# First parameters and last reads on two DMA queues, last rows in four groups, row tables of the last stage on GpSimd

## The chip, the cores and the metric

The kernel runs on one core of a Trainium2 chip. The metric is the time of one execution on the device, in microseconds, and its median over the runs. A core has five engines that work side by side: TensorE (PE; its weight loads are PEld), VectorE (DVE), ScalarE (ACT), GpSimd (POOL) and SyncE (SP). SP issues transfers, ACT can issue them too; sixteen DMA engines carry them out.

## The reference, cut to what matters

```python
def reference(A_u, ..., gate_w):                 # x = A_u: [1, 2048, 640], bf16
    x = A_u
    g = sigmoid((x * gate_w).sum(-1, keepdims=True))
    a = A_ref(x, ...)                            # long convolution, below
    b = (gelu(x @ w_gate) * (x @ w_up)) @ w_down # w_gate, w_up: [640, 1728]
    return g * a + (1 - g) * b

def A_ref(u, A_re, A_im, B_re, B_im, C_re, C_im, log_dt, Dskip):   # [640, 128] each
    dt = exp(log_dt)[:, None]
    logdA, dB = dt * (A_re + 1j * A_im), dt * (B_re + 1j * B_im)
    P = exp(logdA[:, :, None] * arange(2048)[None, None, :])
    K = einsum("dn,dnl,dn->dl", C_re + 1j * C_im, P, dB).real      # one filter per channel
    y = irfft(rfft(u, 4096) * rfft(K, 4096))[:2048]                # along the sequence
    return y + u * Dskip
```

## The kernel before, in words

The kernel does four things at once on five engines, and a written list sets the order.

**The filter.** `A_log_dt` and six parameter tables (`AreT`, `AimT`, `CreT`, `BreT`, `CimT`, `BimT`, 160 KB each) are loaded; ACT makes `dtT` = exp(`ldtT`) (L494), DVE makes `aT` (L495), `aN` (L737) and `bK` (L497). From these ACT makes exponentials (`exps1`, L647; `exps2`, L675) and sines (L633) of phases that DVE computes (`phases`, L624, L626, L628); DVE multiplies them into two grids (L661 to L662, L679, L685), and PE contracts the grids into the filter (`contract`, L711). This is done for each half of the 640 channels (`kgen(0)`, `kgen(1)`), and the result goes to the DRAM tile `dS`.

**The transforms.** The convolution is a Fourier transform in two stages of matrix products. The tables of sines and cosines, `WA`, `TB` and, for the last stage, `WAT`, are made by ACT from integer phases. The phases need per-partition numbers (row numbers with their bits in another order), which DVE computes from the partition number in single-column instructions: `fields` (L367, used by all), `rows` (L387, for `WA`) and `last_rows` (L400, for `WAT`). `WAT` itself comes from an iota on POOL (L949), a DVE instruction (L950) and ACT (L952). The first stage of the input is L776 (16 blocks `un`, results to the DRAM tile `dU`), that of the filter L840 (its rows gathered from `dS` by L804 and L812, results to `dKA`). The second stage is `stageB` (L867), in eight pieces `c` of four columns. `product` (L888) multiplies the two spectra, and `inverse` (L899) transforms each piece back and writes it to the DRAM tile `dY` (L907). `dY` has three parts: `dY[0]` (64 rows) holds the pieces 0 to 3, `dY[1]` (32 rows) 4 and 5, `dY[2]` (32 rows) 6 and 7.

**The last stage** is `finish` (L910). Eight tiles `g` of four columns are read back from `dY` (L913), each in three transfers, since the partitions of a tile come from three parts of `dY`: every second partition from part 0 (320 KB), every fourth from 1 and 2 (160 KB each). Per tile there are two output blocks `ph`. For each, PE does eight products (L922) and DVE computes `z = ps * g + z` (L927). Each tile is then written out in two transfers (L931).

**The feed-forward part.** `gate` (L544 on PE, gelu on ACT L548), `up` (L564 on PE, product on DVE L568) and the down projection `downs` (L592, 28 products for one of sixteen blocks, evicted with the scale 1 - g by L261 or L265), in two groups of 1024 rows. The weights come in blocks of 160 KB through three buffers each (L465), the input `xT` in four loads of 640 KB (L468). Each PSUM result has a pair of banks of its own, of which there are four.

**What sets the order.** Every step is added to a plan (`add`, L98) with its engine, what it reads and writes, and a cost and a rank, which are notes for a planner and aren't used in the kernel. `emit` (L130) goes through the list `ORDER` (L27). One number holds the step, its engine and its pair of PSUM banks:

```python
            s = self.steps[v // 20]
            s["eng"] = ("PE", "DVE", "ACT", "POOL", "SP")[v % 20 // 4]
            s["k"] = 2 * (v % 4)
```

So `ORDER` fixes the order on each engine, and whether an eviction runs on ACT (L259, L261) or DVE (L263, L265). All transfers are issued by SP (`dma`, L242), each engine and SP in the order of the list: an issue that waits holds up all that stand behind it on that queue.

At the end of the list SP issues the writes of pieces 0 to 4, the eight reads of part 0, the writes of the pieces 7, 5 and 6, then the sixteen reads of parts 1 and 2, mixed, and sixteen output writes. PE's last down projections stand between the last inverses; two stand behind the last of them, ahead of L922.

Of the kernel before, what the change touches and what calls it, by code (L numbers as in the profile page):

```python
# [8 lines left out]
ALU = mybir.AluOpType  # L9
# [18 lines left out]
    12 336 6316 316 536 436 516 396 1432 24 376 692 676 988 416 496 476 456 356 616 1004 576 636 1564 556 44 1628  # L28
    656 736 936 596 1064 816 756 2740 1608 64 956 776 716 836 876 1104 1588 796 916 1044 976 2861 1024 896 2836 84
    856 1648 1664 2982 2956 2768 1084 4383 1724 3076 3008 104 2780 2888 1164 1688 4404 1124 1442 1501 2856 2903 1144  # L30
    2804 1748 1784 2976 3020 2924 128 3096 1208 1464 6323 9384 6362 1496 1524 6436 1704 3341 1556 4428 1188 1228
    6388 6348 3436 3222 3044 3368 6416 1764 3103 3316 3248 1808 3380 3196 4444 1844 6441 3456 3262 6468 3404 1868
    1824 6481 3336 3700 6556 6508 3128 6536 1244 3461 3796 3284 3728 144 3143 3556 3488 1884 1268 6562 3216 6600
    3581 6676 6588 6628 1284 168 6656 1304 3822 3676 1324 1344 3608 3500 3916 3848 6721 3576 6748 6682 6796 1364
    6708 4181 3524 6776 1388 3164 3942 4276 4208 1404 2124 6840 4036 6803 3968 3861 6916 6868 2184 6828 2008 3622
    6896 3936 1904 3740 3696 2088 2024 3884 1928 6963 3816 3764 6921 6988 7036 2104 2048 3980 3644 6948 2064 1968
    4063 7016 1944 4056 4004 2148 4222 1984 4156 184 7081 264 4296 7040 2208 7156 2244 7108 7068 4301 2224 288 7136
    208 4088 224 4376 4244 7200 4328 7163 7224 4102 7276 7188 4344 248 7256 2164 4176 4124 2268 7280 2304 7323 4501
    7396 7348 7308 2284 7376 2328 2364 4702 4528 9484 2388 7443 7400 2344 4661 7516 7428 7468 2404 9508 7496 9544
    4728 2420 4688 9604 7523 2444 7562 7548 2461 7636 7588 7616 2503 2484 7640 2524 7682 7668 2541 7756 7708 4580  # L40
    2564 9408 7736 7803 9468 4604 7762 4461 7876 7784 7824 9524 9448 7856 2580 2622 9788 4743 4484 2644 9428 9804
    2604 9828 2716 7881 4764 7922 2676 4620 7996 7904 7948 2736 2696 9844 9908 7976 9748 9924 8556 4543 4644 9868
    8436 8376 9764 8236 8456 9568 9884 8576 8516 8536 8416 8256 8041 4564 8476 8002 4900 8496 8024 8116 8068 8316
    9664 9628 8296 8096 5023 8396 4996 8336 9584 8276 4928 8356 4782 5116 5048 9644 8121 4876 4808 8160 5063 8148
    8188 9688 9944 8216 5382 5136 5141 5476 5084 9968 9704 8620 5236 8583 8608 8648 4823 10064 5408 8676 4940 4896
    5168 4844 10004 8682 5016 8721 8708 5423 8748 8776 4964 10028 5182 5496 5444 9984 5261 5256 5204 10088 8820
    10124 5356 8783 5742 8808 8848 5503 5288 10184 5836 8876 5620 5768 5596 9724 11236 5528 11016 10044 8921 5648
    5716 5302 8948 10104 10148 8883 5324 5376 5540 8904 8976 5781 5564 5616 10208 10164 11322 11283 5856 11020 11348
    11304 11048 8982 5804 9023 9008 5660 9048 10224 9076 11142 11456 10241 5684 11168 5736 11243 11362 10264 10360
    11268 11388 9083 10384 9121 9108 11582 9144 11460 11608 11103 11484 11061 9176 11128 11542 11676 11564 11500  # L50
    11088 10323 12116 11524 9182 10344 9221 9208 10280 9248 9276 11682 11803 10304 11656 11721 11708 11416 11748
    11216 12242 11824 11196 12200 12268 12121 11636 12224 9283 11436 12148 9322 11896 9304 9348 10400 10441 10424
    9376 12163 11762 10468 12184 6080 11788 10536 10496 11856 10516 11876 5861 6108 12316 12296 10556 5983 5956 5888
    12616 12756 6122 6008 6076 11900 11941 6144 11983 11928 11968 12020 12004 5902 12476 12048 12336 13176 13216
    13256 13236 6161 5924 13336 13436 13196 13376 5976 12663 12620 6188 6242 12684 13296 13516 12644 13416 13356
    12724 13276 12343 13496 12481 6268 12704 12520 12096 13316 12364 12508 13396 13456 6284 12548 12383 6201 13476
    12408 12896 12584 13036 12076 12424 13620 12444 13522 13648 13563 13544 13588 12800 12828 12564 13723 13616
    13662 13748 6224 12760 14556 13688 12943 12964 12788 13081 13716 13042 13108 13064 12900 13763 14336 12928 13821
    13124 13862 13788 6020 12984 13888 13816 13144 13848 13004 13916 13963 10892 14642 6044 13921 13988 13948 14683
    14664 14560 14708 14601 14016 14584 14916 14462 14628 14343 14776 14484 14368 14020 14061 14048 10904 14123  # L60
    14382 14148 14084 14160 14188 14263 14404 14116 14221 14288 15180 14216 14244 14962 14756 15208 15263 14736
    14984 14921 15288 14316 15500 14944 14422 15528 10643 14444 10928 12844 14536 14516 12864 10952 15004 14781
    14820 10668 15024 10842 15376 15056 14848 10964 15696 14808 16016 10988 14884 14864 15823 10864 15420 15381
    15848 16656 15404 15102 15448 15063 16336 15124 15088 15581 15700 15608 15464 15743 10562 16976 15728 15164
    15768 15144 15804 15784 15484 15221 10588 15860 15244 15303 15888 15622 15324 16021 15648 15540 16044 15568
    16063 15356 16342 17296 16088 16364 15940 15676 15901 15968 16383 16104 10682 15928 16404 15996 16444 16424
    16124 16140 10704 16221 16168 16183 16244 16262 16208 17340 16284 17368 17021 16463 17048 16484 16500 16316
    16542 16528 16581 16564 16663 16608 16700 16684 16862 16728 16636 16781 16884 17303 16808 10720 17324 17384
    17676 17756 16764 17736 17404 17696 17656 16744 17716 17422 10748 17616 17541 17444 17503 17636 17568 16900
    17524 17182 16928 17461 17204 17103 17488 16820 17124 16982 16848 17596 10601 17004 16956 17084 17064 17143  # L70
    10624 17220 17168 10762 17244 17276 17796 17916 10801 10784 17856 17876 17776 17936 17996 17976 17956 18016
    18056 10824 17836 18083 18076 18120 18104 17816 18036 18144 18202 17896 18241 18563 18224 18196 18600 18176
    18264 18482 18504 18441 18316 18296 18464 18682 18624 18961 18556 18536 18584 18920 18944 18363 18676 18656
    18704 18720 18744 18802 18824 18320 18796 18776 18984 18842 18864 19036 19016 18384 18916 18896 18344 18416
    18436
# [81 lines left out]
def kernel(  # L157
# [72 lines left out]
    def mm(n):  # L230
        return n / 2.28 + 4
# [10 lines left out]
    def dma(kb, fn, r=(), w=(), rank=5.0, run=1280, **k):  # L242
        return add({"SP": 450}, lambda s: fn(), r, w, rank=rank, lat=1900, x=max(100, kb * (3.7 if run < 1000 else 3.3 if run < 2500 else 2.9)), **k)
# [94 lines left out]
    dY = [dp.tile([n, 32, D], BF16, name=f"dY{q}") for q, n in enumerate((64, 32, 32))]  # L338
# [24 lines left out]
    pool(2800, iotas, w=["iot", "ones", "ci"])  # L363

    FIELDS = ((0, 1), (1, 15), (5, 1), (1, 31), (1, 1), (2, 31), (0, 127), (2, 1), (3, 15), (1, 63), (4, 7), (3, 1))

    def fields():  # L367
# [5 lines left out]
        v.tensor_copy(out=ff[:, 0:12], in_=fi[:, 0:12])  # L373
# [7 lines left out]
    B0, B1, B2, B3, P1, P2, P3, P4 = [ff[:, c:c + 1] for c in (0, 4, 7, 11, 9, 5, 8, 10)]  # L381

    def select(v, out, cond, a, b):
        v.tensor_scalar(out=sc8[:, 15:16], in0=a, scalar1=b, scalar2=None, op0=ALU.subtract)
        v.tensor_scalar(out=out, in0=sc8[:, 15:16], scalar1=cond, scalar2=b, op0=ALU.mult, op1=ALU.add)
# [14 lines left out]
    def last_rows():  # L400
        v = nc.vector
        v.tensor_scalar(out=sc8[:, 8:9], in0=B1, scalar1=8.0, scalar2=P4, op0=ALU.mult, op1=ALU.add)
        v.tensor_scalar(out=sc8[:, 8:9], in0=sc8[:, 8:9], scalar1=16.0, scalar2=None, op0=ALU.add)
        select(v, sc8[:, 6:7], B0, sc8[:, 8:9], P3)
        select(v, sc8[:, 9:10], B0, B3, B2)
        select(v, sc8[:, 10:11], B0, B2, B1)
        v.tensor_scalar(out=sc8[:, 9:10], in0=sc8[:, 9:10], scalar1=1024.0, scalar2=8.0, op0=ALU.mult, op1=ALU.add)
        v.tensor_scalar(out=sc8[:, 6:7], in0=sc8[:, 6:7], scalar1=32.0, scalar2=sc8[:, 9:10], op0=ALU.mult, op1=ALU.add)
        v.tensor_scalar(out=sc8[:, 3:4], in0=sc8[:, 10:11], scalar1=-16384.0, scalar2=16384.0, op0=ALU.mult, op1=ALU.add)
# [631 lines left out]
```

## Time and profile before

| What | Value |
|---|---|
| runs, us | 313.37, 312.61, 317.1, 313.4, 313.98, 311.93 |
| their median | 313.38 us |
| profiled execution | 311.22 us, span 309.4 us |
| busy, share of the span | PE 84%, DVE 80%, ACT 72%, POOL 2% |
| granted clock of TensorE, mean | 0.95 |
| DMA | 60.62 MB in 45859 packets, mean 196 GB/s, 61.1% of 16 engines' span, all on one queue |
| loads of ACT's function tables | 26, of 1283 ns each |
| first matmul | 10.34 us |
| last write of `dY`: issued, landed | 280.68, 285.92 us |
| last L927 ends, last output lands | 305.14, 308.55 us |

The profile is that of one execution, and times in it count from the start of its span; the median of the runs is 2.2 us above it. L12 means line 12 of the kernel. SPq is SP issuing transfers, "issue" time in which an engine waits for nothing that the profile shows.

### The profile page before, as it was taken

The page shows a single profiled execution, that of the slowest core. Times are in us where ns is not written, and L with a number is a line of the kernel's source. Part 1 is how long each engine was busy: PE and PEld are TensorE (multiplying, and loading weights), DVE is VectorE, ACT ScalarE, POOL GpSimd, SP SyncE. Part 2 cuts the span into 40 slices and gives each one's busy share as a digit, 9 for nine tenths or more (in the row PEclk, how much of TensorE's full clock was granted, in tenths as well). Part 3 has the DMA queues.
Part 4 walks back from the last instruction along what each step waited for, and adds up shares of the span by engine and source line. Part 5 has one row for each costly group of instructions (what it writes and reads, how often), then busy time and mean ns, then how long its engine had stood idle before and what let it go on. Part 6 is the DMA issues. An engine that isn't in the chain of part 4 may idle for free.

```text
span 309.4 us, 6162 instructions
## 1 busy us (share of the span) xinstructions
PE 259.8 (84%) x2446; PEld 142.0 (46%) x2446; DVE 247.3 (80%) x373; ACT 222.2 (72%) x274; POOL 5.2 (2%) x17
## 2 busy tenths in 40 slices
PE   0698899898599899996899986998578989999461
PEld 0253344343257766742444455343233656666230
DVE  3999999999999939689999875626859799983494
ACT  2999999999998779999888954853468745640000
POOL 4000000000000000000000000000001100000000
PEclk9999999999689999999999999899969999999875
DMA  6995344444241312646334758897599796799886
GB/s 197 386 301 168 106 142 132 131 129 129 85 127 67 106 67 66 173 111 196 103 109 148 254 154 298 280 366 208 165 324 324 264 272 203 268 271 345 256 235 171
DMA packets 45859, 60.62 MB, mean 196 GB/s; under 512 B 4803, under 2 KB 38150, under 8 KB 45830
## 3 DMA queue, kind: packets, MB, share of 16 engines
q1 hardware_dynamic: 45830, 60.23, 61.1%
q8 instruction: 19, 0.31, 0.4%
q14 instruction: 10, 0.08, 0.1%
HBM read 35.80 MB, written 19.17 MB: 178 GB/s over the span
## 4 chain that ended last, share of the span: by engine, by line
PE 42%; DMA 13%; DVE 11%; SPq 7%; ACT 4%; issue 3%; DVEq 0%; ACTq 0%
PE ps L544 13%; PE ps L592 10%; PE ps L564 9%; DMA arena<-dU 4%; PE ps L711 3%; ACT arena L259 3%; SPq L804 3%; DMA dY<-arena 3%; DVE arena L685 3%; SPq L913 3%; DMA arena<-dKA 2%; PE ps L867 2%; DVE arena L568 2%; DVE arena L263 2%; PE ps L899 2%
## 5 line engine op out<-in xcount | busy, mean ns | idle before, releaser
L259 ACT CAST arena<-ps 128x640 bf16<-128x640 f32 (+1 forms) x110 | 70.6, 695 | 33.6 <-PE ps L867 9.8
L544 PE MATMUL ps<-arena 128*128 128x512 bf16 x280 | 67.5, 399 | 16.6 <-DMA arena<-in_w_gu_dram 11.6
L592 PE MATMUL ps<-arena 128*128 128x320 bf16 x448 | 63.1, 299 | 0.0
L263 DVE CAST arena<-ps 128x640 bf16<-128x640 f32 (+3 forms) x62 | 50.5, 848 | 14.4 <-PE ps L711 5.8
L564 PE MATMUL ps<-arena 128*128 128x512 bf16 x260 | 59.7, 380 | 2.6 <-ACT arena L259 0.8
L544 PEld LDWEIGHTS <-arena 128*128 128x128 bf16 x280 | 28.1, 101 | 52.4 <-DMA arena<-in_w_gu_dram 12.0
L592 PEld LDWEIGHTS <-arena 128*128 128x128 bf16 x448 | 43.0, 98 | 18.0 <-issue 0.8
L633 ACT ACTIVATE arena<-arena 128x2560 bf16<-128x2560 int16 x18 | 41.6, 2334 | 1.4 <-DVE arena L628 1.1
L568 DVE TENSOR_TENSOR arena<-ps,arena 128x1024 bf16<-128x1024 f32 x26 | 31.6, 1220 | 12.8 <-PE ps L564 12.7
L564 PEld LDWEIGHTS <-arena 128*128 128x128 bf16 x260 | 25.4, 99 | 32.4 <-issue 3.5
L548 ACT ACTIVATE arena<-ps 128x1024 bf16<-128x1024 f32 (+1 forms) x28 | 27.3, 1023 | 9.3 <-PE ps L544 9.2
L888 DVE TENSOR_TENSOR arena<-arena 128x1280 bf16<-128x1280 bf16 x32 | 24.5, 819 | 2.2 <-DMA arena<-arena 1.9
L867 PE MATMUL ps<-arena 64*64 64x320 bf16 x256 | 17.8, 334 | 6.9 <-DVE arena L263 2.0
L647 ACT ACTIVATE arena<-arena 128x640 bf16<-128x640 f32 x32 | 21.0, 748 | 1.3 <-DVE arena L737 1.3
L265 DVE TENSOR_SCALAR arena<-ps,omg 128x640 bf16<-128x640 f32 x10 | 8.8, 882 | 11.0 <-PE ps L592 11.0
L626 DVE SCALAR_TENSOR_TENSOR arena<-arena 128x320 int32<-128x320 f32 x40 | 16.9, 486 | 0.0
L675 ACT ACTIVATE arena<-arena 128x320 bf16<-128x320 f32 x40 | 16.3, 511 | 0.0
L927 DVE SCALAR_TENSOR_TENSOR arena<-ps,g_f,arena 128x640 bf16<-128x640 f32 x16 | 13.2, 878 | 3.7 <-PE ps L922 3.6
L840 PE MATMUL ps<-arena 128*128 128x320 bf16 x64 | 13.5, 336 | 3.1 <-DMA arena<-dS 2.1
L867 PEld LDWEIGHTS <-arena 64*64 64x64 bf16 x256 | 8.1, 109 | 17.4 <-issue 10.0
L628 DVE TENSOR_SCALAR arena<-arena 128x1280 int32<-128x1280 int32 x18 | 14.9, 827 | 0.6
L711 PE MATMUL ps<-arena 128*64 128x40 bf16 x640 | 11.7, 186 | 3.7 <-issue 3.1
(105 smaller groups left out, 227.8 us busy)
## 6 DMA issues: line engine op xcount, KB each, us to landing
arena<-in_w_gu_dram SPq DMA_DIRECT2D x52, 160.0 KB, 2.5
dU<-arena SPq DMA_DIRECT2D x16, 320.0 KB, 2.4
dKA<-arena SPq DMA_DIRECT2D x16, 320.0 KB, 4.2
arena<-dU SPq DMA_DIRECT2D x8, 640.0 KB, 4.8
arena<-arena SPq DMA_DIRECT2D x16, 320.0 KB, 3.4
arena<-dKA SPq DMA_DIRECT2D x16, 320.0 KB, 4.3
dY<-arena SPq DMA_DIRECT2D x8, 640.0 KB, 5.4
arena<-in_u_nat_dram SPq DMA_DIRECT2D x16, 160.0 KB, 2.3
```

The costliest lines, as they stand in the source:

```text
L259: nc.scalar.copy(out=dst, in_=src(b))
L263: nc.vector.tensor_copy(out=dst, in_=src(b))
L544: nc.tensor.matmul(ps[:, k + j, :], lhsT=Wg[w][:, kt, :], rhs=xT[2 * grp + j][:, kt, :], start=(kt == 0), stop=(kt == NKT - 1))
L548: add({"ACT": an(1024) + 60}, lambda s: nc.scalar.activation(out=HTall[0:p, :, f, :], in_=ps[0:p, plan.bank(g):plan.bank(g) + 2, :], func= ...
L564: nc.tensor.matmul(ps[:, k + j, :], lhsT=Wu[w][:, kt, :], rhs=xT[2 * grp + j][:, kt, :], start=(kt == 0), stop=(kt == NKT - 1))
L568: add({"DVE": v1(1024)}, lambda s: nc.vector.tensor_tensor(out=HTall[:, :, f, :], in0=ps[:, plan.bank(u):plan.bank(u) + 2, :], in1=HTall[: ...
L592: nc.tensor.matmul(ps[:, k + h, 0:W], lhsT=HTq[q][:, f, 128 * j:128 * j + 128], rhs=Wd[f][:, W * h:W * h + W], start=(f == 0), stop=(f == ...
L633: ac(an(8 * W) + 90, lambda: nc.scalar.activation(out=t[:], in_=ph.bitcast(I16)[:, :, :, 0:16:2], func=ACT.Sin, scale=SIN_SCALE), r=[f"ph{ ...
L647: nc.scalar.activation(out=out, in_=ab, func=ACT.Exp, scale=float(4 + 8 * i))
L711: nc.tensor.matmul(ps[64 * y:64 * y + 64, k + i // g, 40 * (i % g):40 * (i % g) + 40], lhsT=cs1[:, x, 80 * y + k0 + i, :], rhs=cs2[:, x, 8 ...
L867: nc.tensor.matmul(ps[64 * y:64 * y + 64, k + x, 0:W], lhsT=TB[64 * x:64 * x + 64, m, :], rhs=t[64 * x:64 * x + 64, 2 * a + y, HV[h]], sta ...
L888: ve(v2(W * CS), lambda x=x: nc.vector.tensor_tensor(out=x[:, :, HV[h]], in0=x[:, :, HV[h]], in1=t, op=ALU.mult), r=ks, w=[k for k in kx i ...
```

## The change

Seven things change.

1. `dma` takes a list of engines that may issue the transfer. `ldtT`, `AreT` and `AimT` are issued by ACT, ahead of all its work. The reads of the last group of rows and the outputs may be issued by SP or ACT.
2. `dY` has four parts, of 64, 32, 16 and 16 rows: pieces 0 to 3, 4 and 5, 6, and 7. The reads cover several tiles each: part 0 in four transfers of two tiles (640 KB), part 1 in two of four (640 KB), part 2 in two of four (320 KB), part 3 in four, of one, one, two and four tiles (80, 80, 160, 320 KB).
3. `last_rows` runs on POOL, with 18 instructions for 11, and `fields` has two more columns; the order of the bits in the rows follows the four parts.
4. `last_rows` has scratch columns of its own, and `rows` no longer writes the key `lrow`.
5. Costs that only the planner reads are other numbers.
6. `ORDER` is another list, 940 steps for 952. SP's first issues are `xT1`, `xT0`, `Wg0`, `un`, `Wu0`, `CimT` (before: `AreT`, `un`, `ldtT`, `BimT`, `Wu0`, `CimT`, `xT0`, `Wg0`). On DVE `rows` comes ahead of L495, on POOL `last_rows` ahead of the iotas of L949. ACT's work changes function tables 24 times (before 26); by step 475, the phases of the second half, it is 14 (before 16). 71 evictions are on DVE (before 72) and 117 on ACT (before 116). Between 20 and 270 us the order is the same in outline, with neighbours exchanged.
7. The end of the list: SP issues the writes of pieces 0 to 4, four reads of part 0, the writes of pieces 7, 6 and 5, then two reads of part 3 (tiles 1 and 0), two of part 2 and two of part 1 (tiles 4 to 7, then 0 to 3 each time), then eight outputs; ACT issues two reads of part 3 (tiles 2 and 3, then 4 to 7) and eight outputs. On PE three down projections stand behind the last inverse. L922 begins with tile 7.

```diff
-    def dma(kb, fn, r=(), w=(), rank=5.0, run=1280, **k):
-        return add({"SP": 450}, lambda s: fn(), r, w, rank=rank, lat=1900, x=max(100, kb * ...), **k)
+    def dma(kb, fn, r=(), w=(), rank=5.0, run=1280, q=("SP",), **k):
+        def go(s):
+            queue[0] = nc.scalar if s["eng"] == "ACT" else nc.sync
+            fn()
+
+        return add({e: 450 for e in q}, go, r, w, rank=rank, lat=1900, x=max(100, kb * ...), **k)
+
+    queue = [nc.sync]
...
-    dY = [dp.tile([n, 32, D], BF16, name=f"dY{q}") for q, n in enumerate((64, 32, 32))]
+    dY = [dp.tile([n, 32, D], BF16, name=f"dY{q}") for q, n in enumerate((64, 32, 16, 16))]
...
     def last_rows():
-        v = nc.vector
-        v.tensor_scalar(out=sc8[:, 8:9], in0=B1, scalar1=8.0, scalar2=P4, op0=ALU.mult, op1=ALU.add)
...
+        v = nc.gpsimd
+        s_, hi, lo = sc8[:, 6:7], sc8[:, 9:10], sc8[:, 10:11]
+        x, y = sc8[:, 12:13], sc8[:, 14:15]
+        v.tensor_scalar(out=x, in0=B2, scalar1=4.0, scalar2=P5, op0=ALU.mult, op1=ALU.add)
+        v.tensor_scalar(out=x, in0=x, scalar1=24.0, scalar2=None, op0=ALU.add)
+        v.tensor_scalar(out=y, in0=P4, scalar1=16.0, scalar2=None, op0=ALU.add)
+        for out, p7, p1, p0 in ((s_, x, y, P3), (hi, B4, B3, B2), (lo, B3, B2, B1)):
+            select(v, y, B1, p7, p1, 13)
+            select(v, out, B0, y, p0, 13)
...
-    ve(2000, last_rows, r=["fld"], w=["lrow"], rank=P["T2"])
+    pool(5000, last_rows, r=["fld"], w=["lrow"], rank=P["T2"])
...
-    dma(160, lambda: nc.sync.dma_start(out=ldtT[:], in_=A_log_dt.partition_broadcast(N)), w=["ldtT"], rank=0)
+    dma(160, lambda: queue[0].dma_start(out=ldtT[:], in_=A_log_dt.partition_broadcast(N)), w=["ldtT"], rank=0, q=("ACT",))
     for i, nm in enumerate(names[:2]):
-        dma(160, lambda i=i, nm=nm: nc.sync.dma_start(out=prT[nm][:], in_=params[i]), w=[nm], rank=0.1)
+        dma(160, lambda i=i, nm=nm: queue[0].dma_start(out=prT[nm][:], in_=params[i]), w=[nm], rank=0.1, q=("ACT",))
...
-        q = max(0, c // 2 - 1)
-        s0 = CS * (c - (0, 4, 6)[q])
+        q = (0, 0, 0, 0, 1, 1, 2, 3)[c]
+        s0 = CS * (c - (0, 4, 6, 7)[q])
...
-    def finish(tiles, R):
-        for q, (p0, st, cs) in enumerate(((0, 2, (0, 1, 2, 3)), (1, 4, (4, 5)), (3, 4, (6, 7)))):
-            for g, (t, nm) in enumerate(tiles):
-                dma(640 // st, lambda t=t, g=g, q=q, p0=p0, st=st: nc.sync.dma_start(out=t[p0:128:st], in_=dY[q][:, 4 * g:4 * g + 4, :]),
-                    r=[("dY", c) for c in cs], w=[(nm, q)], rank=R + P["F0"] * (2 - q), run=5120, odd=True)
+    def finish(tiles, wide, R):
+        rows = ((0, 2, (0, 1, 2, 3), (2, 2, 2, 2)), (1, 4, (4, 5), (4, 4)), (3, 8, (6,), (4, 4)), (7, 8, (7,), (1, 1, 2, 4)))
+        for q, (p0, st, cs, gs) in enumerate(rows):
+            g = 0
+            for n in gs:
+                dst = wide[g // 4][p0:128:st, 4 * (g % 4):4 * (g % 4 + n), :]
+                dma(640 // st * n, lambda dst=dst, g=g, n=n, q=q: queue[0].dma_start(out=dst, in_=dY[q][:, 4 * g:4 * (g + n), :]),
+                    r=[("dY", c) for c in cs], w=[(tiles[j][1], q) for j in range(g, g + n)], rank=..., run=5120, odd=True,
+                    q=("SP", "ACT") if q == 3 else ("SP",))
+                g += n
...
-                    r=[(f"zt{g // 4}", 2 * (g % 4) + b) for b in range(2)], rank=R, run=2560)
+                    r=[(f"zt{g // 4}", 2 * (g % 4) + b) for b in range(2)], rank=R, run=2560, q=("SP", "ACT"))
```

## The prediction

> **What bounds the kernel now.** I first read the busy time by stage, then what each engine waits for at the start, then the chain that ended last.
>
> In the table of windows the columns are window, length, busy time (count) of PE, PEld, DVE, ACT, POOL, the granted clock, the DMA share and GB/s:
>
> ```profile
> 0.00:6.00 6.00, 0.00 (x0) 0.00 (x0) 1.74 (x20) 1.49 (x2) 3.13 (x15) 1.00 0.59 156
> ...
> 20.00:60.00 40.00, 37.33 (x228) 17.49 (x225) 38.80 (x51) 39.75 (x39) 0.00 (x0) 1.00 0.49 151
> 60.00:102.00 42.00, 37.50 (x199) 19.77 (x197) 39.22 (x61) 40.32 (x51) 0.00 (x0) 0.92 0.34 105
> ...
> 276.00:284.30 8.30, 8.30 (x74) 5.72 (x72) 4.03 (x6) 0.69 (x1) 0.00 (x0) 1.00 1.00 340
> 284.30:294.30 10.00, 5.91 (x48) 3.81 (x48) 4.07 (x6) 0.00 (x0) 0.00 (x0) 0.88 0.85 258
> 294.30:309.40 15.10, 5.58 (x42) 2.71 (x38) 10.13 (x13) 0.00 (x0) 0.00 (x0) 0.61 0.75 202
> ```
>
> There are three regimes. Up to 6 us little runs. From 20 to 102 us ACT is the fullest engine (39.75 of 40, 40.32 of 42), DVE close behind, PE at 89 to 93%. At the end the engines wait for transfers, and then DVE works alone. The start is set by one wait, seen in the timelines of ACT and DVE:
>
> ```profile
> 0.74 1.28 ACT L494 ACT_TABLE_LOAD   x1 [0.74 <-PEq L1027]
> 5.80 0.74 ACT L494 ACTIVATE arena<-arena 128x640 bf16<-128x640 bf16 x1 [3.77 <-DMA arena<-in_A_log_dt_dram]
> 7.79 10.40 ACT L647 ACTIVATE arena<-arena 128x640 bf16<-128x640 f32 x16 [1.25 <-DVE arena L737]
> ```
> ```profile
> 6.57 0.82 DVE L495 TENSOR_TENSOR arena<-arena 128x640 f32<-128x640 bf16 x1 [3.79 <-ACT arena L494]
> ```
>
> ACT waits 3.77 us for `ldtT`, which SP issues third, at 1.67 us; DVE waits 3.79 us behind it. The end is in the chain of waits (start, length, what) and in the timelines of SP and DVE:
>
> ```profile
> 275.63 8.66 DMA dY<-arena
> ...
> 284.31 0.47 SPq L913
> ...
> 293.09 4.25 DMA arena<-dY
> 297.35 0.04 issue
> 297.39 1.02 PE ps L922 x12
> ```
> ```profile
> 284.31 10.02 SPq L913 DMA_DIRECT2D arena<-dY  x16
> ```
> ```profile
> 287.31 0.88 DVE L265 TENSOR_SCALAR arena<-ps,omg 128x640 bf16<-128x640 f32 x1 [2.92 <-PE ps L592]
> 290.90 1.68 DVE L927 SCALAR_TENSOR_TENSOR arena<-ps,g_f,arena 128x640 bf16<-128x640 f32 x2 [2.71 <-PE ps L922]
> 292.88 1.68 DVE L927 SCALAR_TENSOR_TENSOR arena<-ps,g_f,arena 128x640 bf16<-128x640 f32 x2 [0.31 <-PE ps L922]
> 295.01 3.26 DVE L927 SCALAR_TENSOR_TENSOR arena<-ps,g_f,arena 128x640 bf16<-128x640 f32 x4 [0.46 <-PE ps L922]
> 298.44 6.70 DVE L927 SCALAR_TENSOR_TENSOR arena<-ps,g_f,arena 128x640 bf16<-128x640 f32 x8 [0.17 <-PE ps L922]
> ```
>
> After the writes of `dY` have landed, SP alone issues sixteen reads, one per 0.64 us, until 294.3 us. In that stretch the DMA engines move 258 GB/s, just before it 340. So the last reads are paced by their issue. DVE starts its sixteen L927 at 290.90 and ends at 305.14 us: 13.32 us busy in 14.24.
>
> **The change, part by part.**
>
> *First parameters on ACT's queue.* `ldtT` is now ACT's first issue, at about 0.75 us, with `AreT` and `AimT` behind it. No ACT-issued transfer is in this trace, so I bound it. The Exp cannot come before 0.74 + three issues at SP's first rows (0.41 to 0.43) + the table load of 1.28 = 3.3 us; with the 4.1 us that `ldtT` was in flight before (1.67 to 5.80), it comes at 4.9. I take 4.5, nearer to the transfer's own row: 1.3 us earlier (0.9 to 2.5). The two later issues hide behind that flight.
>
> *SP's order.* `xT1`, `xT0` and `Wg0` come first. PE's first matmul waited for `Wg0` until 10.34 us, with 1760 KB issued up to it (page, DMA issues); now it is 1920 KB, in two queues, so PE gains between 0 and 2.3 us (a landing at 8.0, if the bytes flow from the first transfer on at the 348 GB/s of 6 to 20 us).
>
> *ACT's tables.* The new order changes function tables 24 times, not 26 (the trace has 26 loads of 1283 ns). Both savings lie before 102 us: 2 x 1.283 = 2.6 us. ACT gains 1.3 + 2.6 = 3.9 us.
>
> *Row tables.* `rows` (13 instructions, 7.67 to 10.44 us, 2.77 us) moves ahead of L495 into the wait, of which 2.5 us are left. `last_rows` (11 instructions, 2.44 us) leaves DVE; on POOL it is 18 instructions. POOL's own small rows last 0.11 to 0.29 us, so 2.0 to 5.2 us; the wait of L949 behind it is 228 us, so even ten times that costs nothing. The two added instructions of `fields` (0.14 us) lie in the same DVE wait. DVE gains 1.3 + 2.5 + 2.4 less one eviction of 0.88 that it takes over early = 5.3 us.
>
> [...]
>
> *Sum of the start.* ACT is the tightest engine and caps the gain at 3.9 us; PE has 7.2 us of idle time in 20 to 102 us to give, but 0 is its floor. I take **3.0 us** (0 to 3.9), close to the ACT rows, since ACT is the engine at 96 to 99%.
>
> *The middle, 102 to 276 us.* The same work in a locally permuted order; one eviction moves from DVE to ACT (0.85 against 0.70 us). I cost it at nothing, within 2 us either way.
>
> *The last reads.* Sixteen issues become eight: six on SP, two on ACT. ACT has no work then. PE has three down projections (3.98 us each) behind the last inverse, not two. So the last write of `dY`, issued at 280.68 us, comes 3.9 us earlier, 276.8, lands 5.24 us later as that one did, at 282.0, and the last rows' first half (640 KB) needs the 2.45 us of a 160 KB read plus 480 KB at 340 GB/s, 1.45 us: about 286 us. That is before PE is free (287.27). Then PE and the eviction at 287.31 + 0.88 are late next, and DVE starts L927 at 288.2, not 290.90: 2.7 us. All tiles come close together, so the 0.92 us of gaps between DVE's sixteen go: 0.9. PE needs 0.73 to 0.77 us for a tile's half against DVE's 0.84, so it hides; if it does not, 16 x the difference is due. After DVE's last instruction two output issues stand in a row; on two queues one, 0.5 us, goes. Sum: 4.1 us.
>
> The lower end: if the last write lands as now (285.92), the first half comes at 285.95 + 3.9 + 1.9 (the 640 KB issued just before it) = 291.8 us, later than the 290.3 at which PE now starts, because whole halves are waited for where now one tile sufficed. DVE then starts at 292.1: 1.2 lost, 0.9 and 0.5 won, 0.2 us. I take **3.0 us**, a quarter of the way from the upper end, because the order of the down projections speaks for early writes.
>
> The row of 258 GB/s against 340 says that issue is what the end waits for. [...]
>
> Total: 311.2 - 3.0 - 3.0 = 305.2 us against the profiled execution (311.22, span 309.4). The median of the runs, 313.38, lies 2.2 above that execution, so the forecast for the median is **307.4 us**.
>
> **Rivals.** *Start only:* the writes land late and the halves arrive after 291 us; the end gives 0.2. For it: DMA share 1.00 from 276 to 284 us. Against: the write is issued 3.9 us earlier. 313.4 - 3.0 - 0.2 = 310.2 us.
>
> *End only:* what ACT wins is lost by 200 us, where PE, DMA and SP's gathers (0.64 us each) are in the chain. For it: ACT is idle 17 us of the 40 from 200 to 240 us. Against: everything there starts from data made earlier. 313.4 - 3.0 = 310.4 us.
>
> *No change:* waits from the permuted order eat both gains, 6 us; for it, 197 to 245 us has SP in order with copies between the gathers. 313.4 us.
>
> *Slower:* the last two groups write 16 partitions each. If such a transfer fills fewer than 16 engines, its 1280 KB run slower: at half the engines + 3.9 us at 340 GB/s (311.3 us), at a quarter + 11.6, **319.0 us**. It decides below a third of the rate, where the 6 us and the 1.6 of the bound are used up. For it: no read of 5 KB rows into 16 partitions is in the trace. Against: the reads into 32 partitions land in the same 2.4 to 2.9 us as others of that size.
>
> [...]
>
> **How the numbers follow.** Forecast 0.56 (307.4), start only 0.14, end only 0.12, no change 0.10, slower 0.08. 0.5% is 1.6 us, about what a measurement of this kernel tells from no change. Faster are the first three, less 0.01 for their upper edges: 0.81; same 0.11; slower 0.08. The range: low from both upper ends (3.9 + 4.1 = 8.0, 305.4) less the 1.4 us by which the fastest run lies under the median, 304.0; high takes in both 310 cases and 2 us of the middle, 312.4. Outside are no change and slower, 0.18.
>
> **What would show it.** Start: the Exp at 4.5 us, L647 near 6.5, 24 table loads, `rows` ahead of L495; wrong if the Exp stays near 5.8. End: eight L913 issues on SP and ACT; the first L927 about 2.7 us nearer to PE's last L592 than now (3.6), sixteen of them without gaps; wrong if PE's L922 still waits for `dY` for 3 us or more, or if the last write's landing isn't earlier against PE's end. Middle: the stages between 102 and 276 us equally long.

## The result and the profile after

The changed kernel is slower: the ratio to the kernel before is **1.0096 [1.0076, 1.0117]**, about 3.0 us; the medians of all runs are 315.73 us (28 runs) and 313.83 us (63 runs), 1.9 us or 0.6% apart. The ratio is one of fast runs alone, those within 1.5% of a kernel's fastest, which here are all 28 of the changed kernel and 40 of the 63 of the kernel before, so the loss lies between 0.6 and 1.0%. 307.4 us was forecast. The profiled execution of the changed kernel took 315.16 us (span 313.4) at a mean granted clock of 0.919, the lowest among its runs (0.93 to 0.953 in the others), and the profile of before is one of its shorter executions (311.22 us), so the two profiles stand 4.0 us apart.

The windows of the changed kernel, columns as in the prediction:

```profile
0.00:6.00 6.00, 0.00 (x0) 0.00 (x0) 4.18 (x35) 1.28 (x1) 4.74 (x21) 1.00 0.59 148
...
20.00:60.00 40.00, 38.07 (x235) 18.01 (x234) 34.52 (x53) 38.13 (x37) 0.00 (x0) 0.87 0.48 144
60.00:102.00 42.00, 39.00 (x205) 20.40 (x205) 38.09 (x52) 36.83 (x49) 0.00 (x0) 0.96 0.36 114
...
284.30:294.30 10.00, 8.92 (x66) 6.19 (x64) 2.65 (x3) 0.00 (x0) 0.00 (x0) 1.00 1.02 280
294.30:313.40 19.10, 10.21 (x64) 5.02 (x64) 13.32 (x16) 0.00 (x0) 0.00 (x0) 0.56 0.55 172
```

ACT, at 99 and 96% before in the second and third row, is at 95 and 88%: it is no longer the fullest engine and waits more. The granted clock of the second row is 0.87 (before 1.00).

The start, from the timelines of ACT, DVE and PE, first two lines of the kernel before that the prediction doesn't show:

```profile
19.50 2.85 ACT L548 ACTIVATE arena<-ps 128x1024 bf16<-128x1024 f32 x3
10.34 9.17 PE L544 MATMUL ps<-arena 128*128 128x512 bf16 x30 [10.34 <-DMA arena<-in_w_gu_dram]
```
```profile
0.73 0.40 ACTq L463 DMA_DIRECT2D arena<-in_A_log_dt_dram  x1
1.17 0.92 ACTq L465 DMA_DIRECT2D arena<-in_params_dram  x2
6.65 0.74 ACT L502 ACTIVATE arena<-arena 128x640 bf16<-128x640 bf16 x1 [3.24 <-DMA arena<-in_A_log_dt_dram]
9.98 10.48 ACT L655 ACTIVATE arena<-arena 128x640 bf16<-128x640 f32 x16 [2.60 <-DVE arena L745]
22.40 1.03 ACT L556 ACTIVATE arena<-ps 128x1024 bf16<-128x1024 f32 x1
```
```profile
8.77 0.82 DVE L503 TENSOR_TENSOR arena<-arena 128x640 f32<-128x640 bf16 x1 [3.27 <-DMA arena<-in_params_dram]
```
```profile
10.11 6.06 PE L552 MATMUL ps<-arena 128*128 128x512 bf16 x20 [10.11 <-DMA arena<-in_w_gu_dram]
18.94 3.30 PE L552 MATMUL ps<-arena 128*128 128x512 bf16 x10 [2.77 <-DMA arena<-in_w_gu_dram]
```

`ldtT` is issued 0.94 us earlier and lands 0.83 us later, in flight 5.9 us, not 4.1. DVE's product behind the Exp then waits for `AreT`, which takes 7.5 us, and PE stops for `Wg1`, which SP now issues at 13.12 us (before 7.02) and which lands at 18.89 (before 13.22). The first gelu (L556) begins at 22.40 us, 2.9 later than before (19.50).

The end, from the timelines of PE and DVE and the chain of waits, first PE in the kernel before:

```profile
279.49 7.78 PE L592 MATMUL ps<-arena 128*128 128x320 bf16 x56
290.32 0.73 PE L922 MATMUL ps<-arena 128*64 128x320 bf16 x8 [3.05 <-DMA arena<-dY]
```
```profile
281.63 11.58 PE L600 MATMUL ps<-arena 128*128 128x320 bf16 x84
295.22 1.28 PE L935 MATMUL ps<-arena 128*64 128x320 bf16 x16 [2.00 <-DMA arena<-dY]
```
```profile
295.72 13.58 DVE L940 SCALAR_TENSOR_TENSOR arena<-ps,g_f,arena 128x640 bf16<-128x640 f32 x16 [1.51 <-PE ps L935]
```
```profile
282.71 5.08 DMA dY<-arena
287.80 7.37 DMA arena<-dY
```

The last write is issued 2.0 us later than before (282.71 against 280.68). The merged read behind it takes 7.4 us, so the first L940 starts at 295.72 (before L927: 290.90), and then all sixteen run without a gap.

PE's last down projection ends at 293.21 us, before at 287.27: 5.9 us later. From there to the end of the last of the sixteen it takes 16.09 us, before 17.87: 1.8 us less. So in these two executions the end gains, and the loss is made ahead of it.

### The profile page after: what moved, and what is told of

Its sections match the earlier page's. It is cut to its first block, busy times and chain, and to the rows that moved or that the text cites. A ratio compares the mean times of both kernels' runs of the same rounds, so it can differ in the third digit from the quotient of the medians.

```text
span 313.4 us, 6178 instructions
## 1 busy us (share of the span) xinstructions
PE 267.9 (85%) x2446; PEld 143.3 (46%) x2446; DVE 244.3 (78%) x363; ACT 220.2 (70%) x273; POOL 11.5 (4%) x35
## 4 chain that ended last, share of the span: by engine, by line
PE 48%; DMA 17%; DVE 11%; ACT 11%; SPq 7%; issue 3%; ACTq 0%; DVEq 0%
PE ps L572 13%; PE ps L552 13%; PE ps L600 11%; SPq L812 4%; ACT arena L264 4%; DVE arena L268 4%; DMA arena<-in_B_w_down_dram 3%; DMA arena<-in_params_dram 3%; DMA arena<-dY 2%; DVE arena L940 2%; DMA arena<-dS 2%; PE ps L719 2%; PE ps L875 2%; PE ps L848 2%; DMA arena<-dU 2%
## 5 line engine op out<-in xcount | busy, mean ns | idle before, releaser
L552 PE MATMUL ps<-arena 128*128 128x512 bf16 x280 | 66.4, 393 | 14.8 <-DMA arena<-in_w_gu_dram 12.9
L572 PE MATMUL ps<-arena 128*128 128x512 bf16 x260 | 65.5, 411 | 1.3 <-ACT arena L264 0.7
L600 PE MATMUL ps<-arena 128*128 128x320 bf16 x448 | 63.0, 299 | 0.4 <-DVE arena L270 0.3
L268 DVE CAST arena<-ps 128x640 bf16<-128x640 f32 (+3 forms) x61 | 49.7, 849 | 11.6 <-PE ps L875 5.4
L600 PEld LDWEIGHTS <-arena 128*128 128x128 bf16 x448 | 43.3, 98 | 18.8 <-issue 1.9
L552 PEld LDWEIGHTS <-arena 128*128 128x128 bf16 x280 | 27.6, 100 | 50.0 <-DMA arena<-in_w_gu_dram 14.2
L572 PEld LDWEIGHTS <-arena 128*128 128x128 bf16 x260 | 27.1, 105 | 36.5 <-issue 10.8
L556 ACT ACTIVATE arena<-ps 128x1024 bf16<-128x1024 f32 (+1 forms) x28 | 27.4, 1024 | 9.7 <-PE ps L552 9.6
L875 PE MATMUL ps<-arena 64*64 64x320 bf16 x256 | 18.8, 333 | 6.7 <-ACT arena L264 2.9
L784 PE MATMUL ps<-arena 128*128 128x320 bf16 x64 | 12.0, 310 | 7.7 <-DVE arena L634 5.3
L848 PE MATMUL ps<-arena 128*128 128x320 bf16 x64 | 13.8, 335 | 3.0 <-DMA arena<-dS 2.1
L940 DVE SCALAR_TENSOR_TENSOR arena<-ps,g_f,arena 128x640 bf16<-128x640 f32 x16 | 13.3, 879 | 1.8 <-PE ps L935 1.5
```

The costliest lines, as they stand in the source:

```text
L268: nc.vector.tensor_copy(out=dst, in_=src(b))
L552: nc.tensor.matmul(ps[:, k + j, :], lhsT=Wg[w][:, kt, :], rhs=xT[2 * grp + j][:, kt, :], start=(kt == 0), stop=(kt == NKT - 1))
L556: add({"ACT": an(1024) + 60}, lambda s: nc.scalar.activation(out=HTall[0:p, :, f, :], in_=ps[0:p, plan.bank(g):plan.bank(g) + 2, :], func= ...
L572: nc.tensor.matmul(ps[:, k + j, :], lhsT=Wu[w][:, kt, :], rhs=xT[2 * grp + j][:, kt, :], start=(kt == 0), stop=(kt == NKT - 1))
L600: nc.tensor.matmul(ps[:, k + h, 0:W], lhsT=HTq[q][:, f, 128 * j:128 * j + 128], rhs=Wd[f][:, W * h:W * h + W], start=(f == 0), stop=(f == ...
L848: nc.tensor.matmul(ps[:, k + ri, 0:W], lhsT=WA[:, ph, ri, :], rhs=Kl[:, ph, :], start=True, stop=True)
```

## The experiments

Ratios are to the kernel before, run beside each on the same chip. Of a change to `ORDER` the diff gives the order on the queues that move.

**1. The start alone, the end alone.** My theory after the result: the first loads on two queues share the DMA engines and so all come late, and the merged reads make PE wait for whole halves. The rival for each was that it costs nothing and the loss lies in the middle. x1 is the kernel before with the new first loads:

```diff
-SP: AreT, un, ldtT, BimT, Wu0, CimT, xT0, Wg0, ...
+ACT: ldtT, AreT, AimT
+SP: xT1, xT0, Wg0, un, Wu0, CimT, ...
```

> The kernel before, with the first loads alone as in the change: ldtT, AreT and AimT issued by ACT, SP's first 31 loads in the changed order; all else as before. Theory 'sharing': ACT's three small loads share the DMA engines with SP's 640 KB loads, so ldtT lands near 6.6 us and AreT near 8.7, the first L647 starts near 10 us (before 7.8), and this lasts to the end: ratio to before 1.006 to 1.013. Rival 'order': the loss of the change comes from the permuted order of the middle; then the ratio is 0.998 to 1.003 here, whatever the first microseconds show. The forecast's own view (the loads gain 1.3 us) would give 0.996 or less.

x4 is the kernel before up to the last inverses, with the changed end:

```diff
-    dY parts 64, 32, 32; reads of parts 1 and 2: sixteen of one tile, SP
+    dY parts 64, 32, 16, 16; reads merged as in the change, SP and ACT
```

> The body of the kernel before with the end of the change: four parts of dY, reads in merged transfers on SP and ACT, outputs on both queues, row tables of the last stage on GpSimd. Down projections, writes of dY and all first loads stand as before (two down projections behind the last inverse; the reads of part 1 are issued ahead of those of part 2, since piece 6 is written last here). The forecast's view: 2 to 3 us less, ratio 0.990 to 0.994, the first L927 (here L940) at most 290 us. Rival 'halves': a tile can't start before the whole 640 KB half of part 1 has landed, the first L940 starts at 291 to 293 us, its sixteen run without gaps, and the ratio is 0.998 to 1.004.

Measured: x1 1.0117 [1.0059, 1.0175], x4 1.0108 [1.0065, 1.0152]. PE of x1 at the start, and of x4 at the end:

```profile
10.44 4.45 PE L551 MATMUL ps<-arena 128*128 128x512 bf16 x10 [10.44 <-DMA arena<-in_w_gu_dram]
18.65 5.95 PE L551 MATMUL ps<-arena 128*128 128x512 bf16 x20 [3.76 <-DMA arena<-in_w_gu_dram]
```
```profile
280.45 7.78 PE L601 MATMUL ps<-arena 128*128 128x320 bf16 x56
294.92 3.15 PE L936 MATMUL ps<-arena 128*64 128x320 bf16 x24 [6.69 <-DMA arena<-dY]
```

Each part by itself loses over 1%, together 2.2%, more than the whole change loses (0.96%). So something else in the change gains about 1%. With two down projections behind the last inverse (7.78 us) PE is idle for 6.69 us; before, the first L927 came 3.6 us after PE's last L592. In x4 piece 6 is written last, so the reads that PE waits for there go into 16 partitions (below); what merging alone costs x4 doesn't tell.

**2. The start mended.** x2 puts the three parameters back on SP, now first of all; x3 leaves them on ACT and moves `gwc`, whose 640 packets of two bytes stood ahead of the weights `Wg2` and `Wg1`, behind `xT2`; x5 does both. x12 and x14 are x2 and x5 a second time.

```diff
-ACT: ldtT, AreT, AimT
-SP: xT1, xT0, Wg0, un, Wu0, CimT, drow, gwc, ...
+SP: ldtT, AreT, AimT, xT1, xT0, Wg0, un, Wu0, CimT, drow, ..., xT2, gwc
```

> The changed kernel, with ldtT, AreT and AimT issued first on SP, ahead of xT1, xT0 and Wg0, and nothing on ACT's queue at the start. Theory 'sharing': ldtT lands by 4.5 us, AreT by 5.5, the first L647 starts by 7.5 us instead of 9.98, the first matmul still near 10 us since the same 1920 KB stand ahead of it; ratio to before 0.998 to 1.003, so 2 to 3.5 us less than the change. Rival 'order': the time stays at 1.008 to 1.011, since PE's wait for the third weight block sets the start and the middle's order the rest.

> The changed kernel, with the load of gate_w (640 pieces of 2 bytes) moved on SP from place 8 to behind xT2. In the changed kernel's trace its pieces hold the DMA engines at 57 to 106 GB/s from 9.5 to 11 us. Theory 'small pieces': Wg1 and xT2 land about 1.2 us earlier, PE's 2.77 us wait before the third gate shrinks by about that, and the time falls by 0.5 to 1.5 us (ratio 1.005 to 1.008). Rival 'sharing' alone: ACT starts no earlier, no gain, 1.008 to 1.011.

> The changed kernel with the three parameters first on SP and the gate's two-byte load behind xT2; end as changed. Theory (both costs of the start are separate and add: 0.4% for the parameters on the second queue, 0.4% for the early two-byte pieces): 0.999 to 1.004 of the kernel before, Exp near 5.1 us, PE without a wait over 1 us before 20 us. Rival (they are the same lost time, each mend takes back only what the other would): 1.004 to 1.007.

> x2 once more, on the chip of these runs: x2 and x3 each gave back 0.4% and both together (x5, another chip) 2%. Theory (the two mends help each other, since the exponentials and the first weights must both be there): 1.003 to 1.008 as x2. Rival (the difference lies between chips or in chance): 0.990 to 0.998.

> x5 once more (start mended, end as changed). Theory (the two start mends together are worth 1.5% or more of the changed kernel): 0.986 to 0.995. Rival (they are worth 0.8%, the sum of x2 and x3): 0.999 to 1.004. The end by halves still costs: 0.002 or more above x13.

Measured: x2 1.0059 [1.0019, 1.0099], x12 1.0006 [0.997, 1.0041]; x3 1.0058 [1.0015, 1.0101]; x5 0.9895 [0.9841, 0.9948], x14 0.9998 [0.9957, 1.0039]. ACT and PE in x14:

```profile
4.07 0.74 ACT L503 ACTIVATE arena<-arena 128x640 bf16<-128x640 bf16 x1 [2.06 <-DMA arena<-in_A_log_dt_dram]
6.62 5.94 ACT L656 ACTIVATE arena<-arena 128x640 bf16<-128x640 f32 x9 [1.82 <-DVE arena L746]
```
```profile
9.54 9.39 PE L553 MATMUL ps<-arena 128*128 128x512 bf16 x30 [9.54 <-DMA arena<-in_w_gu_dram]
```

One queue with the small loads first gives the Exp at 4.07 us (4.06 to 5.14 in the eleven profiles with this start), for which I had forecast 4.5 on two queues, and in this profile the thirty gate products follow each other; the first gelu is at 19.05 us. Either mend alone returns 0.4% (x2, x3) or 0.9% (x12, the program of x2), and the intervals of x2 and x3 overlap that of the changed kernel. Both mends together return about 1% (1.0096 to 0.9998). x5, with six runs, came out 1% lower than its repetition; its profile is one without the half-speed stretch of experiment 5, that of x14 has it. Whether that is the difference isn't shown. No run has the parameters on ACT's queue beside SP's old order, so the two are not separated.

**3. The end mended.** x6 keeps the changed start. The group written last (pieces 4 and 5) is read tile by tile, from SP and ACT in turn, and PE takes the tiles in that order. x7 has this end and x5's start; x13 is x7 again.

```diff
-... (1, 4, (4, 5), (4, 4)), (3, 8, (6,), (4, 4)), (7, 8, (7,), (1, 1, 2, 4)))
+... (1, 4, (4, 5), (1,) * 8), (3, 8, (6,), (4, 4)), (7, 8, (7,), (4, 4)))
```

> The changed kernel with its start; at the end the last group (pieces 4 and 5) is read tile by tile from SP and ACT in turn, the two 16-row groups in halves, and TensorE takes the tiles in that order. Theory (the merged halves make TensorE wait, 2.5 us in the changed kernel): the wait before the first of the sixteen falls under 0.5 us and the ratio to 1.001 to 1.004. Rival (16-row groups move at some 200 GB/s whatever is merged behind them, so that the tiles arrive no earlier): TensorE waits as long in sum, spread over the tiles, 1.007 to 1.011.

> Both mends in one: start as in x5, end as in x6. Theory (the order between start and end gains about 1%, and both ends took it back): 0.990 to 0.996, and the sixteen follow the last down projection without a wait. Rival (no gain in the order): 0.999 to 1.003.

> x7 once more (both ends mended), on the chip of these runs. Theory (both losses are real and the rest of the change gains): 0.985 to 0.994. Rival (x7 owed its time to its chip or to the granted clock of its six runs): 0.996 to 1.002.

Measured: x6 0.9996 [0.9949, 1.0043], 1.0% under the changed kernel; x7 0.9886 [0.983, 0.9941]; x13 0.9906 [0.9857, 0.9956], 0.9% under x14. So by the ratios the end mend is worth 0.9 to 1.0% with either start. The medians of x13 and x14, run on one chip, are 311.84 and 312.96 us, 0.4%, and the profiles say the same: from PE's last down projection to the last of the sixteen it takes 14.5 us in x6 and in x13, 16.09 in the changed kernel and 15.4 in x14. So it is worth 0.3 to 1.0%. The wait was to fall under 0.5 us and fell to 1.25 (x6), here the PE of x6:

```profile
282.16 11.58 PE L601 MATMUL ps<-arena 128*128 128x320 bf16 x84
294.99 1.28 PE L936 MATMUL ps<-arena 128*64 128x320 bf16 x16 [1.25 <-DMA arena<-dY]
```

The rival of 16-row groups that hold up what stands behind them is thus not dead: the tiles still arrive late. x18 takes those groups away: three groups as before, the pieces 6 and 7 one group of 32 rows, all else as x13 (the row tables are those of before, on GpSimd). x17 is x13 with all outputs on SP.

```diff
-    dY parts 64, 32, 16, 16; (3, 8, (6,), (4, 4)), (7, 8, (7,), (4, 4))
+    dY parts 64, 32, 32;     (3, 4, (6, 7), (4, 4))
```

> x13 with the last rows in three groups as before (pieces 6 and 7 are one group of 32 rows, read in halves once piece 6 has landed), row tables of before on GpSimd; the group of pieces 4 and 5 still by tiles, two queues. Theory (the two 16-row groups move slower than 32-row ones, so that their earlier start is worth nothing): ratio within 0.003 of x13's (0.988 to 0.996), wait before the sixteen under 2 us. Rival (the fourth group's earlier reads are what keeps the end short): wait 3 us or more, 0.998 or above.

> x13 with all sixteen outputs issued by SP, none by ACT. Theory (the forecast's 0.5 us for the second queue at the end: only the very last output is issued later): last product to end 0.3 to 0.7 us longer, ratio 0.001 to 0.003 above x13's (0.990 to 0.996). Rival (outputs pile up on one queue and the last lands over 1 us later): 0.004 or more above x13's.

Measured: x18 **0.9857 [0.9802, 0.9913]**, faster than both kernels; x17 0.9931 [0.9893, 0.9969], 0.25% above x13, less than the intervals can tell; from the last of the sixteen to the span's end x17 takes 3.97 us and x13 3.92. PE of x18 at the end:

```profile
279.65 11.58 PE L598 MATMUL ps<-arena 128*128 128x320 bf16 x84
291.18 1.56 PE L933 MATMUL ps<-arena 128*64 128x320 bf16 x16
```

The wait is gone. The windows from 288 to 292 us, first of the changed kernel, then of x18:

```profile
288.00:292.00 4.00, 4.00 (x32) 2.87 (x30) 0.88 (x1) 0.00 (x0) 0.00 (x0) 1.00 1.02 227
```
```profile
288.00:292.00 4.00, 4.00 (x36) 2.88 (x35) 1.01 (x2) 0.00 (x0) 0.00 (x0) 1.00 0.92 360
```

At a DMA share of 1.02, all engines busy, the 16-row reads move 227 GB/s; x18's reads 360 at 0.92. In the trace's packets a row of 20 KB takes 1.2 to 1.6 us in the 16-row reads; in the 32-row reads that follow, the first 16 rows take 0.9 to 1.3 us and the other 48 0.77. These 32-row reads begin at 292.0 us, though their write landed at 287.79: until then the engines are at the 16-row reads, issued ahead of them. So the fourth group gains nothing by starting earlier; that it costs time is likely (0.9857 against 0.9906), but the two intervals overlap.

**4. Order, tables and the third down projection.** x8 is the program of before with only the list changed: the new order between start and end, mended start, reads and outputs of before. x9 is x8 with `last_rows` on GpSimd. x10 (and x15, the same again for its profile) is the kernel before with the parameters first on SP and `gwc` three places earlier, directly behind `xT2`. x11 has the order of before, the mended start and the end by tiles. x16 is x13 with one down projection moved ahead of the last inverse.

```diff
 x9 against x8
-DVE: fields, rows, last_rows, L496
+DVE: fields, rows, L496
+POOL: last_rows
 x16 against x13, PE
-..., inverse 7, down, inverse 4 and 5, down, down, down, L936
+..., inverse 7, down, down, inverse 4 and 5, down, down, L936
```

> The program of before (one queue, three row groups, row tables on VectorE) with only the written order changed: between start and end the order of the changed kernel, with the parameters first and the two-byte load late, and at the end the reads, products and outputs in the order of before, with three down projections behind the last inverse instead of two. Theory (start +1.2%, end +1.1%, so the order must gain 1.3%): 0.986 to 0.993. Rival (the third down projection covers what the late reads cost, the costs don't add, and the order gains nothing): 0.998 to 1.003.

> x8 with its eight instructions of the last stage's row tables on GpSimd instead of VectorE; everything else as x8 (order of the changed kernel, parameters first, end of before). Theory (in this order the tables stand ahead of the first product on VectorE, 2.2 us that every later exponential and gelu waits for): first gelu 2 us or more earlier than in x8 (under 19.6 us), ratio 0.990 to 0.997. Rival (the difference between x8 and x5 is made at the end, by the two queues and four groups): 1.000 to 1.005.

> The kernel before with one thing changed: the three parameters first on SP, the rest of its order untouched (the two-byte load directly behind xT2). The start term of the forecast by itself. Theory (an earlier Exp carries to the end one for one): Exp 1 to 1.7 us earlier, first gelu as much, 0.991 to 0.997. Rival (VectorE's row tables and the exponentials take the time back, or TensorE's clock does): 0.998 to 1.002.

> x10 once more, for its profile: the kernel before with the parameters first on SP and nothing else changed. Theory (an earlier Exp carries through): 0.991 to 0.997, first gelu near 18.2 us. Rival: 0.998 to 1.002.

> The order of before between start and end, the parameters first on SP, and at the end four row groups on two queues with the group written last (piece 6) read tile by tile. With x7, x9 and x10 it makes a square of order and end, all with the mended start. Theory (order and end each gain about 0.6%): 0.992 to 0.998, above x7 by 0.004 or more. Rival (the order gains nothing, only start and end count): 0.986 to 0.991, as x7.

> x7 with one down projection moved from behind the last inverse to ahead of it (two behind, as in before). Theory (the third down projection covers the last write and reads; what the order gains at the end is this): the last write is issued 3.9 us later, TensorE waits 4 to 5.5 us before the sixteen instead of 0.9, ratio 1.010 to 1.015 above x13's. Rival (the reads are bound by the transfers before them, which start no later): wait under 2.5 us, ratio within 0.006 of x13's.

Measured: x8 1.0056 [1.002, 1.0092]; x9 0.998 [0.9929, 1.0031]; x10 0.9941 [0.9904, 0.9978] and x15 0.9953 [0.9916, 0.999]; x11 1.0005 [0.9962, 1.0047]; x16 1.0051 [1.0011, 1.0091]. PE of x16:

```profile
284.73 7.78 PE L601 MATMUL ps<-arena 128*128 128x320 bf16 x56
298.26 3.99 PE L936 MATMUL ps<-arena 128*64 128x320 bf16 x28 [5.75 <-DMA arena<-dY]
```

- *x8 and x9.* In the new order `last_rows` on DVE stands ahead of the first product, and the first gelu comes at 21.36 us; on GpSimd at 19.59. The tables' move is worth 0.8% (the intervals just meet), but only where the parameters are early, as far as the profile tells; in the changed kernel DVE idles there anyway (3.27 us).
- *x10 and x15.* An Exp 1.3 us earlier (4.54 us) and a first gelu 1.3 us earlier (18.23) gain 0.5 to 0.6% in the old order. That the lead carries to the end rests on these ratios: the profile of x15 is of a longer execution (314.31 us, the median is 312.08), and in it PE's last down projection ends at 289.9 us, before at 287.27.
- *x16.* The third down projection behind the last inverse is worth 1.45% (by the medians, 311.84 and 314.66 us, 0.9%): with it the last write goes out 4.9 us earlier (280.87 in x13 against 285.80) and PE waits 1.24 us, not 5.75. The profile of x16 is of one of its longest executions, 317.61 us.
- *x11.* The same by the other way round: two down projections behind, a wait of 6.23 us, and no gain. Here too piece 6 is written last, so the tiles waited for are 16-row reads, and the order isn't the only difference to x13. x8 failed its theory: the order by itself does not gain 1.3%. Of the four programs with a mended start, the new order is the faster with the end by tiles (x13 against x11) and not with the old end (x9 against x15).

**5. A half-speed stretch.** x7 and x13 are one program, and their profiles differ by 3.3 us. Windows of x7, then of x13:

```profile
22.00:24.00 2.00, 0.99 (x4) 0.48 (x5) 1.61 (x5) 1.97 (x3) 0.00 (x0) 1.00 0.96 279
24.00:26.00 2.00, 2.00 (x11) 0.90 (x10) 0.69 (x1) 2.00 (x2) 0.00 (x0) 1.00 0.83 241
26.00:28.00 2.00, 2.00 (x11) 0.93 (x10) 1.97 (x6) 2.00 (x2) 0.00 (x0) 1.00 0.58 185
```
```profile
22.00:24.00 2.00, 0.70 (x2) 0.37 (x3) 1.73 (x5) 1.97 (x3) 0.00 (x0) 0.50 0.97 291
24.00:26.00 2.00, 2.00 (x5) 0.62 (x5) 0.00 (x0) 2.00 (x1) 0.00 (x0) 0.50 0.76 213
26.00:28.00 2.00, 2.00 (x6) 0.73 (x5) 0.47 (x1) 2.00 (x3) 0.00 (x0) 0.50 0.33 112
```

At a granted clock of 0.50 PE gets through half the matmuls (5 or 6 in 2 us, not 11), and ACT then waits for it, in x13 2.48 us:

```profile
34.93 1.29 ACT L265 CAST arena<-ps 128x640 bf16<-128x640 f32 x2 [2.48 <-PE ps L785]
```

The changed kernel has this from 20.2 to 30.4 us, and ACT waits 1.64 us behind it. The delay stays: PE's last down projection ends 2.9 us later in x14 (with the stretch) than in x5 (without it, the same program), and 3.0 us later in x13 than in x7. The stretch stands in eleven of the fourteen profiles with the new order and, of five with the old, only in x1 (18.2 to 21.6 us, from near the end of its 3.76 us of idle PE). What differs ahead of it: in the old order the 80 products of one column (27 ns each, 2.1 us) are followed at once by the up products. In the new order two small products and a wait for DVE follow first, so that 2.8 to 4.6 us pass between the last gate product and the first up product. In the changed kernel itself the 2.77 us of waiting for `Wg1` end at 18.94 us, 1.2 us ahead of the drop. That is a correlation, and x7 has the same work there as x13 without the drop; a kernel with the up products moved back was not tried.

## Why the prediction was wrong, step by step

The sum had 3.0 us won up to PE's last down projection and 3.0 us behind it. In the two profiles the first part is 5.9 us lost and the second about 2 won, so of the 10 us between the forecast for the profiled execution (305.2) and its time (315.16) some nine lie ahead of the end.

- **Parameters on ACT's queue: the step that failed first.** I took the Exp at 4.5 us from the flight of 4.1 us that `ldtT` had on SP, and called 4.9 the late bound. It came at 6.65. The flight is not the transfer's own: from 2 to 5 us, among the packets of 5120 bytes from SP's queue, a packet of 1280 bytes takes 97 to 169 ns (medians by half microseconds), later 55. The bytes that the new order issues at the same time on SP were in no term. The two later issues did hide behind that flight, but the landing of `AreT`, now behind `ldtT`, was in no term either: DVE waited for it until 8.77. Instead of 1.3 us won, 2.9 us are lost at the first gelu. x1, with these loads alone, loses 1.2%, and the rows of experiment 2 show that the same wish, small loads first, is met on one queue.
- **SP's order.** "PE gains between 0 and 2.3 us" looked at the first matmul only (10.11, before 10.34). The price came at a later block of weights: `Wg1` is issued 6.1 us later than before, 2.77 us of wait.
- **ACT's tables.** 24 loads, as said. What the two saved loads of 1.28 us bring by themselves was not tried.
- **Row tables.** Right in kind: `rows` fits into the wait, POOL hides `last_rows`. It took 7.8 us (3.90 to 11.73) for 18 instructions, 0.43 us each with the gaps between them, not 2.0 to 5.2. The rows of 0.11 to 0.29 us that I took the rate from are other instructions of POOL; these last 0.19 to 0.87.
- **The clock between 20 and 102 us: a term that the sum did not have.** I counted PE's idle time there and took its clock as before. The half-speed stretch costs 2.5 us on PE in the profiled execution (20 up products in 6.98 us, before in 4.49), and x5 against x14 shows that some 3 us of it last to the end. It falls in some executions of a program and not in others, and what brings it on stays open.
- **The middle at nothing, within 2 us.** It held, as far as one profile of each tells: the first half's contraction (L711, now L719) ends 3.7 us later than before (114.67 against 111.00), and the first inverse starts 4.6 us later (242.76 against 238.16), so the stages between lose 0.9 us.
- **The last write 3.9 us earlier.** x16 shows that the third down projection is worth that and more, but I set it on PE's old end of 287.27 us. Start and stretch had made PE late: its last down projection ends at 293.21, and the write is 2.0 us later, not 3.9 earlier. Against PE's end it did move as said: it lands 5.4 us ahead of it, before 1.35.
- **The reads.** DVE was to start its sixteen 2.7 us nearer to PE's last down projection; it starts 2.5 us behind it, before 3.6, so 1.1 of the 2.7 came. My lower end named the reason, "whole halves are waited for where now one tile sufficed". The half waited for took 7.4 us from the landing of its write, not the 3.9 of the sum, and 4.2 of these pass before its first packet, behind the 16-row reads.
- **The sixteen and the outputs.** As said: 13.58 us without gaps (before 14.24), and 3.0 us from the last L940 to the last landing (before 3.4). Whether the second queue did that isn't shown: with all outputs on SP, x17 ends as x13.
- **The rival on the slow side** had a part of the mechanism: 16-row reads do run at 227 GB/s against 340 in the write stretch, two thirds, which by its own sum (half the engines: 3.9 us) would not have decided alone. It rested on 16 rows filling fewer than 16 engines. They fill them (share 1.02); it is each row that is slower, 1.2 to 1.6 us for 20 KB against 0.77 in most rows of the 32-row reads. Why a row is slower there isn't shown.

## What to carry to other kernels

A transfer's flight in the old trace need not hold in other company (`ldtT`: 4.1 us, then 5.9): when loads move to a second queue, price them with all bytes that are issued beside them, and look at the next consumer too. Merging reads saves issues, but the consumer may wait longer for them; where it could begin with one tile, the last-arriving group read tile by tile gained 0.3 to 1.0%, and without the slow 16-row reads ahead of it PE no longer waited (1.24 us in x13, none in x18). Put work that waits for nothing behind the last producer to cover its write and read (a third down projection: a wait of 1.24 us, not 5.75), and count an earlier event from the new end of the engine, not from the old.

## What the runs showed of the hardware

- Reads into 16 partitions, every eighth one, move at 227 GB/s with all DMA engines busy (share 1.02; changed kernel, 288 to 292 us), a row of 20 KB in 1.2 to 1.6 us. Reads into 32, every fourth, move at 360 in the same window of x18 (share 0.92); in the changed kernel most of their rows of 20 KB take 0.77.
- TensorE falls to a granted clock of 0.50 for 10.2 us in the changed kernel (from 20.2 us), 6.8 in x13, 3.4 in x18; 20 up products then take 6.98 us (changed kernel), not 4.49 (before). Ahead of it lie 2.77 us of idle PE in the changed kernel and 80 products of one column (2.1 us) in x13; in x1 it begins near the end of 3.76 us of idle PE. The programs of x13 and x14 have it in those executions and not in those of x7 and x5; its cause isn't shown.
- In the changed kernel 640 packets of two bytes, placed ahead of `Wg2` and `Wg1`, go with 106 and 57 GB/s in the half microseconds from 10 to 11 us, at a DMA share of 0.55 and 0.51; from 9 to 9.5 it was 371 GB/s.
